# Startup and weight-split order in a four-layer SSM/SwiGLU kernel: input loaded first, sines last, and a rewritten row at the end of the kernel stage

## The chip, the cores and the metric

The kernel runs on one core of one Trainium2 chip. The metric is the device time of one execution in microseconds. The kernel before took 1164.55 us, the median of 3 runs (1164.26 to 1165.54).

## The reference

Four layers follow one another on an activation of 2048 rows by 512 channels. Layers 1 and 3 are a state-space convolution, layers 2 and 4 a SwiGLU block; both layers of a kind share their weights.

```python
def _A_ref(u, A_re, A_im, B_re, B_im, C_re, C_im, log_dt, Dskip):
    dt = jnp.exp(log_dt)[:, None]
    logdA = dt * (A_re + 1j * A_im)
    P = jnp.exp(logdA[:, :, None] * l[None, None, :])
    K = jnp.einsum("dn,dnl,dn->dl", Cc, P, dt * Bc).real
    ...
    y = irfft(rfft(u padded) * rfft(K padded))[:L] + u * Dskip
def _B_ref(x, w_gate, w_up, w_down):
    return (_silu(x @ w_gate) * (x @ w_up)) @ w_down
x = x + _A_ref(_layernorm(x), ...)
x = x + _B_ref(_layernorm(x), ...)
x = x + _A_ref(_layernorm(x), ...)
x = x + _B_ref(_layernorm(x), ...)
```

## The kernel before

The program has three parts.

**Startup.** `dt` is the exponential of `log_dt`, made by a polynomial on VectorE (DVE) over 4 columns, spread to all partitions by a diagonal matrix `dg` (L169), one matrix product `pd` (L170) and a copy on ScalarE (ACT, L172). `rho` (L958) is `dt` times the real part of A. The phases are kept as turns: `turn_units` (L373) scales the imaginary part (L379), rounds it on ACT (L380) and subtracts (L382); it runs once for the first 64 channels (`first`) and once for the other 448 (`others`). For one chunk of 64 channels `gen_turns` (L387) makes the phases by shifts and additions, `gen_trig` (L404) their sines and cosines on ACT (`re`, `im`), `gen_exp` (L416) the 25 exponentials `mz` and `re[:, a]`, and `gen_g` (L456) and `gen_e` (L441) multiply these into the two factors of the convolution kernel. `stats` (L196) makes mean and variance of the 4 row groups of block 0 of the input (`xne`) with BN_STATS, the power -0.5 on GpSimd (POOL), and `norm_early` (L287) normalizes them on ACT. `direct` (L292) is the forward transform of a block as fp32 matrix products (L298).

**Kernel stage.** For each of 8 chunks of 64 channels, 128 small products `pk` (`lags`, L498) make the convolution kernel, which is copied (`ks`, L509), spread over the partitions (for the last two chunks by `kp`, L525, on TensorE), given the skip term (`skip`, L505), and transformed into spectra (`spectra`, `first_parts` L582, `later_parts` with the products of L533). At its end stand, for the last chunk, the first convolution block and the preparation of the SwiGLU weights. `ssm_half` (L740) is a generator for one half of the channels: four steps, each a spectrum product on DVE (`yk` L778, `yf` L783 and L784) and an inverse transform on PE (`pi`, L798), with the sums `bb` (L750 on ACT, L758 and L759 on DVE), and two final steps that add the results to the residual rows `xg` (L812 to L831). `conv[0]` and `conv[1]` are the two halves of block 0. `split_weights` (L647) yields for each of 11 weight pieces a load into a staging tile, a `hi` step (fp16 copy on ACT, L666 or L691) and a `lo` step (the fp16 rest on DVE, L671 or L694); `tags` names the staging buffer of each load, where a number is a third of a not yet used weight buffer. `split(hi, lo, load)` takes the next ones of each list. `scales` (L344) computes the power-of-two scales from the largest squares. `second` (L306) is the transform of block 1 by `direct`. `first_norm` (L832) normalizes and transposes (`pt`, L845) the first 256 rows for the SwiGLU block.

**SwiGLU and convolution blocks.** For 8 pairs of layer and block, gate and up products `pgu` (L911 to L914: three fp16 products for each fp32 one, two buffers of PSUM), the gate's SiLU on ACT (L917), the product with up on DVE (L918, `sg`), and the down products `py` (L926 to L928), while DVE, ACT and PE work on the convolution of the next block. The order here is found by the scheduler of the framework, from its own estimates.

In the first two parts the rows of ACT, DVE, PE and POOL are in the order in which the code is written (`manual_schedule`); the DMA queue of SyncE (SP) is put in order by the scheduler at both ends. Each engine takes its row in order, so that an instruction which waits holds up all behind it.

Of the kernel before, what the change touches and what calls it, by code (L numbers as in the profile page):

```python
# [22 lines left out]
P = 128  # L23
# [4 lines left out]
HD = D // 2  # L28
# [46 lines left out]
def kernel(ctx, tc, x, a_re, a_im, b_re, b_im, c_re, c_im, log_dt, d_skip,  # L75
                           w_gate, w_up, w_down, c_ef, c_ei, c_ek, c_am, c_eh, c_eih, out):
    nc = tc.nc
    V, A, G, PE = nc.vector, nc.scalar, nc.gpsimd, nc.tensor
# [9 lines left out]
    def tl(shape, name, tag, dt=F32):  # L88
        return sb.tile(shape, dt, name=name, tag=tag, bufs=BUFS[tag])
# [17 lines left out]
    def load_half(c):  # L107
        nc.sync.dma_start(xe[:, c:c + 2], x[0, c * P:(c + 2) * P, :].rearrange("(c p) d -> p c d", p=P))
    load_half(0)
    rho = load(a_re, "rho", "u")  # L110
    th = load(a_im, "th", "u")
    am = sb.tile([P, NA], I32, name="am")
    nc.sync.dma_start(am, c_am)
    load_half(2)
    bw = tl([P, 2, D], "bw", "nn")
    br, bi = bw[:, 0], bw[:, 1]
    nc.sync.dma_start(br, b_re)
# [75 lines left out]
        V.tensor_reduce(dmax, da, axis=AX.X, op=OP.max)  # L193


    def stats(src, rows, scale, tag="stats", between=None, then=None):  # L196

        st = tl([P, 4, 6], "st", tag)
        mv = tl([P, 4, 2], "mv", tag)
        rs = tl([P, 8], "rs", tag)  # L200
        nb = rs[:, 4:]
        for r in range(rows):
            if between and r == 2:
                between()
            V.bn_stats(st[:, r], src[:, r])
            V.bn_aggr(mv[:, r], st[:, r])
        V.tensor_scalar(rs[:, :rows], mv[:, :rows, 1], EPS, 1.0 / scale ** 2, OP.add, OP.mult)
        G.tensor_tensor(rs[:, :rows], rs[:, :rows], mhalf[:, :rows], OP.pow)
        if then:
            then()  # L210
        V.scalar_tensor_tensor(nb[:, :rows], mv[:, :rows, 0], -1.0, rs[:, :rows], OP.mult, OP.mult)
        return rs, nb
# [191 lines left out]
    def gen_trig(ts):  # L404


        re, im, mu, xz, mz = ts
        A.activation(xz[:, 2], xz[:, 1].bitcast(I32), AF.Sin, scale=-TWO_PI / TURN)
# [222 lines left out]
    def take(it, n):  # L631
        for _ in range(n):
            next(it, None)
# [13 lines left out]
    def split_weights():  # L647


        cb = F // 4  # L650
        tags = iter(("bt", 0, 1, 2, "bt", 0, 1, 2, "n", "xf", "bt"))

        def columns(j, wi, src):
            fs = slice(j * cb, (j + 1) * cb)
# [298 lines left out]
    with tc.manual_schedule(engines={mybir.EngineType.Activation, mybir.EngineType.DVE, mybir.EngineType.PE, mybir.EngineType.Pool}):  # L953
# [3 lines left out]
        def turns():  # L957
            V.tensor_tensor(rho, rho, dt, OP.mult)  # L958
            take(first, 1)
            take(ex, 14)  # L960
            take(others, 1)
            take(first, 1)
            take(gen_turns(0, ts[0]), 7)
        ft = tl([P, 2, 2, D], "ft", "ga")
        first, others = turn_units(ft, 0, DC), turn_units(ft, DC, D)
        stats_x = stats(xe, 4, 1.0, between=turns, then=lambda: take(others, 1))
        tr = gen_trig(ts[0])
        take(tr, 2)
        norm_early(xe, ne, stats_x)
        gen_w()  # L970
        take(ex, 11)
        fw = [direct(0, h, q, [ne[:, c, h * HD:(h + 1) * HD] for c in range(4)]) for h in range(2) for q in QORD]
        for f in fw:
            next(f)
# [171 lines left out]
        xg = tl([P, 2, 4, D], "xg", "gb")  # L1146
        xs[0], xs[1] = xg[:, 0], xg[:, 1]
        wsl += [tl([P, 6 * F], f"wsl{k}", f"W{k}", F16) for k in range(4)]
        load_x(xs[0], 0, 0)
        split(0, 0, 3)  # L1150
        conv = [ssm_half(0, 0, h) for h in range(2)]

        def slots():
# [2 lines left out]
            yield from itertools.cycle([w[:, j] for w in (wz, wm) for j in range(2)])  # L1156
        slots = slots()

        ks = spread_in(pk)
        odd = later_parts(c - 1, kts[0], (3, 1))  # L1160
        rest = later_parts(c, kts[1])
        bb1 = tl([P, 2, 2, 2, HD], "bb1", "n")
        norm = first_norm(tl([P, 2, D], "nn1", "hf"))
        take(conv[0], 1)
        spread_pe(ks, kts[1])
        skip(c, kts[1], V)
        take(conv[0], 1)
        scales()
        split(1, 0)
        first_parts(c, 0)  # L1170
        take(conv[0], 1)
        split(1, 1)
        split(0, 0, 1)
        first_parts(c - 1, 3)
        split(1, 0)
        take(conv[0], 1)
        first_parts(c - 1, 1)
        split(1, 0)
        take(conv[1], 1)
        first_parts(c, 2)  # L1180
        take(conv[1], 1)
        split(0, 1)
        split(0, 0, 1)
        take(conv[0], 1)
        take(conv[1], 1)
        split(1, 1)
        split(0, 0, 1)
        take(conv[1], 1)
        split(0, 1)
        split(0, 0, 1)  # L1190
        take(odd, 2)
        take(conv[1], 1)
        take(norm, 1)
        take(rest, 2)
        take(odd, 1)
        take(norm, 1)
# [11 lines left out]
        take(rest, 3)  # L1208
        split(1, 1)
        take(rest, 4)  # L1210
        split(0, 0, 3)
        sizes(c, kts[1], ks)
        direct_size()
        nn2 = tl([P, 2, D], "nn2", "nn")
        take(second(*sec[-1]), 2)
    pscale = product_scale()
    with tc.high_priority(offset=BOOST // 2):
        while los:
# [50 lines left out]
```

## Time and profile before

| quantity | value |
|---|---|
| median of 3 runs | 1164.55 us |
| the profiled execution | 1163.83 us |
| its span in the trace | 1161.1 us |
| around the span | 2.7 us |
| mean granted TensorE clock | 0.989 |
| first `pk` product | 56.55 us |
| last `pk` product ends, first `pi` starts | 258.5 us |
| first gate product | 318.53 us |

The page gives the busy time of each engine, the timeline the single instructions in order of time (start, length, engine, line, operation; in brackets the idle time before it and what ended it), and the list of waits who waited for whom. A row with "x4" merges four instructions. PE is TensorE.

### The profile page before, as it was taken

To read this page: it belongs to the slowest core of one execution; us is meant where nothing else is said; L and a number is where in the kernel's file an instruction comes from. 1 tells how busy PE (TensorE), PEld (TensorE's weight loads), DVE (VectorE), ACT (ScalarE), POOL (GpSimd) and SP (SyncE) were. 2 spreads that over 40 slices of the span, in tenths; PEclk is the share of its full clock that TensorE was granted. 3 is DMA by queue.
4 is the path that set the end of the run, shared out by engine and by line. 5 is a ranking of instruction groups with operands and counts; after the bars stand their busy time and mean duration, and the time that the engine had idled before them with its cause. 6 is when DMAs were issued, how large, how long until landed. Compare 5 with 4: busy or idle time off the path is not lost.

```text
span 1161.1 us, 24400 instructions
## 1 busy us (share of the span) xinstructions
PE 1101.9 (95%) x9942; PEld 877.3 (76%) x9942; DVE 998.6 (86%) x1586; ACT 599.7 (52%) x1198; POOL 109.7 (9%) x162
## 2 busy tenths in 40 slices
PE   2989999998889999999999999999999999999998
PEld 1868888886776868687868687868777686876875
DVE  7999999968789999999899999989994999983212
ACT  6889898733553463557453533655433452334211
POOL 1112222210000010010010000210000010000000
PEclk9989999998899999999999999999999999999999
DMA  5357677866394437332264444343534145312000
GB/s 208 129 162 164 161 178 175 187 172 226 112 289 119 145 119 222 105 111 74 79 155 134 127 161 145 103 132 88 164 109 150 49 121 158 102 42 46 15 23 19
DMA packets 127314, 150.38 MB, mean 130 GB/s; under 512 B 50897, under 2 KB 75985, under 8 KB 127202
## 3 DMA queue, kind: packets, MB, share of 16 engines
q1 hardware_dynamic: 115298, 123.32, 34.9%
q0 software_dynamic: 11904, 25.50, 9.5%
q8 instruction: 78, 1.28, 0.5%
q14 instruction: 34, 0.28, 0.1%
HBM read 98.70 MB, written 33.82 MB: 114 GB/s over the span
## 4 chain that ended last, share of the span: by engine, by line
DVE 30%; PE 30%; issue 7%; DMA 4%; ACT 3%; SPq 1%; POOL 1%; DVEq 0%; ACTq 0%; POOLq 0%
PE pgu L911 5%; PE pgu L912 5%; PE pgu L914 5%; DVE t L778 5%; DVE yk L781 4%; PE py L926 3%; PE py L927 3%; PE py L928 3%; DVE yk L778 3%; DVE z L230 3%; DVE sg L918 2%; PE pi L798 2%; PE pf L282 2%; DVE hl L920 2%; DMA w<-wdr 2%
## 5 line engine op out<-in xcount | busy, mean ns | idle before, releaser
L911 PE MATMUL pgu<-mix,wsl 128*128 128x256 f16 x1280 | 299.2, 273 | 5.5 <-DVE sg L918 5.0
L912 PE MATMUL pgu<-mix,wsl 128*128 128x256 f16 x1280 | 298.9, 273 | 0.0
L914 PE MATMUL pgu<-mix,wsl 128*128 128x256 f16 x1280 | 195.2, 273 | 0.0
L912 PEld LDWEIGHTS <-wsl 128*128 128x128 f16 x1280 | 125.2, 98 | 22.7 <-issue 6.4
L926 PE MATMUL py<-wsl,hh 128*128 128x512 f16 (+1 forms) x352 | 133.5, 379 | 4.9 <-DVE xg L931 3.0
L911 PEld LDWEIGHTS <-wsl 128*128 128x128 f16 x1280 | 125.1, 98 | 16.4
L914 PEld LDWEIGHTS <-wsl 128*128 128x128 f16 x1280 | 125.2, 98 | 15.3
L928 PE MATMUL py<-wsl,hl 128*128 128x512 f16 (+1 forms) x352 | 133.4, 379 | 0.5 <-DVE hl L920 0.5
L927 PE MATMUL py<-wsl,hh 128*128 128x512 f16 x320 | 121.3, 379 | 0.0
L778 DVE TENSOR_TENSOR t<-uu,w 128x1024 f32<-128x1024 f32 x96 | 116.9, 1218 | 3.5 <-DMA w<-wdr 3.2
L917 ACT ACTIVATE sg<-pgu,sc 128x512 f32<-128x512 f32 x80 | 54.6, 683 | 125.1 <-PE pgu L914 121.8
L781 DVE TENSOR_TENSOR yk<-yk,t 128x1024 f32<-128x1024 f32 x96 | 116.8, 1217 | 0.2
L918 DVE SCALAR_TENSOR_TENSOR sg<-pgu,sc,sg 128x512 f32<-128x512 f32 x80 | 59.6, 745 | 52.1 <-ACT sg L917 51.9
L533 PE MATMUL pw<-kt,ek 128*128 128x256 f32 (+1 forms) x384 | 92.2, 378 | 0.0
L919 ACT ACTIVATE hh<-sg 128x512 f16<-128x512 f32 x80 | 50.1, 627 | 79.5 <-DVE sg L918 79.5
L533 PEld LDWEIGHTS pw<-kt,ek 128*128 128x128 f32 x384 | 73.6, 196 | 8.6
L798 PE MATMUL pi<-yl,mix 128*128 128x256 f16 x576 | 78.9, 273 | 0.6 <-DVE yl L230 0.3
L282 PE MATMUL pf<-z,eh 128*128 128x256 f16 x576 | 74.9, 273 | 0.6 <-DVE z L230 0.6
L778 DVE TENSOR_TENSOR yk<-u,w0r 128x1024 f32<-128x1024 f32 x56 | 68.1, 1217 | 0.8 <-ACT u L284 0.8
L498 PE MATMUL pk<-re,g 128*32 128x64 f32 x1024 | 65.1, 317 | 3.6 <-DMA g<-g 1.9
L920 DVE TENSOR_TENSOR hl<-sg,hh 128x512 f16<-128x512 f32 x80 | 54.9, 686 | 15.5 <-ACT hh L919 15.4
L927 PEld LDWEIGHTS <-hh 128*128 128x128 f16 (+1 forms) x352 | 34.4, 98 | 41.6 <-issue 6.0
(237 smaller groups left out, 2165.9 us busy)
## 6 DMA issues: line engine op xcount, KB each, us to landing
w<-wdr SPq DMA_DIRECT2D x96, 256.0 KB, 2.7
uu<-udr SPq DMA_DIRECT2D x96, 256.0 KB, 3.0
udr<-u POOLq DMA_DIRECT2D x32, 256.0 KB, 2.6
g<-g POOLq DMA_DIRECT2D x6, 1024.0 KB, 9.1
udr<-u SPq DMA_DIRECT2D x16, 256.0 KB, 3.0
n<-xdr SPq DMA_DIRECT2D x4, 1024.0 KB, 5.7
kdr<-ks SPq DMA_DIRECT2D x6, 512.0 KB, 2.6
kt<-kdr SPq DMA_DIRECT2D x24, 128.0 KB, 2.9
```

The source lines that it names most:

```text
L282: PE.matmul(pf[:, o], lhsT=e, rhs=m, start=k == 0, stop=k == len(terms) - 1)
L533: PE.matmul(pw[:, i], lhsT=e, rhs=kt[:, :, c + 4 * k0:4 * k1:4, :].rearrange("p g k d -> p k g d"), start=c == 0, stop=c == 3)
L778: V.tensor_tensor(t, uu.unsqueeze(2).to_broadcast([P, NQ, 2, 2, DC]), w.unsqueeze(3).to_broadcast([P, NQ, 2, 2, DC]), OP.mult)
L781: V.tensor_tensor(yk, yk, t, OP.add)
L798: PE.matmul(pi[:, o], lhsT=e, rhs=m, start=k == 0, stop=k == len(terms) - 1)
L911: PE.matmul(o, lhsT=wgu(wi, k, 0)[:, fs], rhs=nh[:, k], start=k == 0, stop=False)
L912: PE.matmul(o, lhsT=wgu(wi, k, 1)[:, fs], rhs=nh[:, k], start=False, stop=False)
L914: PE.matmul(o, lhsT=wgu(wi, k, 0)[:, fs], rhs=nlo[:, k], start=False, stop=k == 3)
L918: V.scalar_tensor_tensor(sg, pgu[:, 1], sc6[:, 4:5], sg, OP.mult, OP.mult)
L926: PE.matmul(py[:, r], lhsT=hh[:n, f, rc], rhs=wd(f, 0)[:n], start=f == 0, stop=False)
L927: PE.matmul(py[:, r], lhsT=hh[:n, f, rc], rhs=wd(f, 1)[:n], start=False, stop=False)
L928: PE.matmul(py[:, r], lhsT=hl[:n, f, rc], rhs=wd(f, 0)[:n], start=False, stop=f == FT - 1)
```

## The change

Six things are changed, and none adds or drops arithmetic.

1. The second half of block 0's rows is loaded right behind the first, ahead of `rho`, `th` and `am`.
2. `stats` no longer breaks off after two row groups; all four BN_STATS come first and `turns` is called while POOL takes the power.
3. In `turns` all 25 exponentials of chunk 0 are taken at once, and the large part of `turn_units` is begun only behind `gen_turns`. Then come the normalization, `gen_w`, the sines of chunk 0, and the last step of `others`.
4. The staging buffers of the weight loads are dealt out otherwise (the second load gets `n` instead of a third of a weight buffer).
5. `scales` and the first `hi` step stand ahead of the copy of the last `pk`, and the first two pieces' `lo` steps are between the first convolution steps; the others come later than before. The skip term of the last chunk is added on POOL instead of DVE.
6. The last transform of block 1 (`second(*sec[-1])`, 8 products and their copy) stands ahead of the last convolution step instead of at the end of the stage.

```diff
     load_half(0)
+    load_half(2)
     rho = load(a_re, "rho", "u")
...
-    load_half(2)
...
-    def stats(src, rows, scale, tag="stats", between=None, then=None):
+    def stats(src, rows, scale, tag="stats", then=None):
...
-            if between and r == 2:
-                between()
...
-        tags = iter(("bt", 0, 1, 2, "bt", 0, 1, 2, "n", "xf", "bt"))
+        tags = iter(("bt", "n", 0, 1, "bt", 2, 0, 1, "n", "xf", "bt"))
...
         def turns():
             V.tensor_tensor(rho, rho, dt, OP.mult)
             take(first, 1)
-            take(ex, 14)
-            take(others, 1)
+            take(ex, 25)
             take(first, 1)
             take(gen_turns(0, ts[0]), 7)
+            take(others, 1)
...
-        stats_x = stats(xe, 4, 1.0, between=turns, then=lambda: take(others, 1))
-        tr = gen_trig(ts[0])
-        take(tr, 2)
+        stats_x = stats(xe, 4, 1.0, then=turns)
         norm_early(xe, ne, stats_x)
         gen_w()
-        take(ex, 11)
+        take(gen_trig(ts[0]), 2)
+        take(others, 1)
...
+        split(0, 0, 1)
         load_x(xs[0], 0, 0)
-        split(0, 0, 3)
+        split(0, 0, 2)
...
+        scales()
+        split(1, 0)
         ks = spread_in(pk)
...
-        take(conv[0], 1)
-        spread_pe(ks, kts[1])
-        skip(c, kts[1], V)
-        take(conv[0], 1)
-        scales()
-        split(1, 0)
-        first_parts(c, 0)
-        take(conv[0], 1)
-        split(1, 1)
-        split(0, 0, 1)
-        first_parts(c - 1, 3)
+        last = second(*sec[-1])
         split(1, 0)
         take(conv[0], 1)
-        first_parts(c - 1, 1)
-        split(1, 0)
-        take(conv[1], 1)
-        first_parts(c, 2)
-        take(conv[1], 1)
+        split(0, 1)
+        split(0, 0, 1)
+        spread_pe(ks, kts[1])
+        skip(c, kts[1], G)
+        take(conv[0], 1)
         split(0, 1)
         split(0, 0, 1)
         take(conv[0], 1)
+        first_parts(c, 0)
+        split(1, 0)
+        bb1 = tl([P, 2, 2, 2, HD], "bb1", "n")
+        first_parts(c - 1, 3)
+        take(conv[0], 1)
+        first_parts(c - 1, 1)
         take(conv[1], 1)
-        split(1, 1)
-        split(0, 0, 1)
+        first_parts(c, 2)
+        split(1, 0)
         take(conv[1], 1)
-        split(0, 1)
-        split(0, 0, 1)
+        take(conv[0], 1)
+        take(conv[1], 1)
+        split(1, 0)
+        take(last, 2)
+        take(conv[1], 1)
         take(odd, 2)
         take(conv[1], 1)
         take(norm, 1)
+        split(0, 0, 1)
+        split(0, 1)
+        split(0, 0, 1)
...
+        split(0, 1)
         split(0, 0, 3)
...
-        take(second(*sec[-1]), 2)
```

What stands in the rows of the engines, in the built programs (lines of the kernel after are two or three less from L205 on). First ACT at the start, before: `mz` and `re<-rho` are exponentials, `re<-im`, `im<-im` and `re<-re,hpi` the large sines and cosines of chunk 0, `xne` the normalization of block 0.

```order
L426 ACTIVATE re<-rho 128x64 x9
L380 ACTIVATE ft<-ft 128x2x448
L408 ACT_TABLE_LOAD
L408 ACTIVATE xz<-xz 128x320
...
L411 ACTIVATE re<-im 128x2048
L412 ACTIVATE im<-im 128x2048
L413 ACTIVATE re<-re,hpi 128x2048
L290 ACTIVATE xne<-xne,rs 128x512 x4
L426 ACT_TABLE_LOAD
L426 ACTIVATE re<-rho 128x64 x11
```

The same place of ACT's row after:

```order
L424 ACTIVATE re<-rho 128x64 x20
L378 ACTIVATE ft<-ft 128x2x448
L288 ACTIVATE xne<-xne,rs 128x512 x4
L406 ACT_TABLE_LOAD
L406 ACTIVATE xz<-xz 128x320
...
L409 ACTIVATE re<-im 128x2048
L410 ACTIVATE im<-im 128x2048
L411 ACTIVATE re<-re,hpi 128x2048
```

Eleven exponentials and the four normalizations have moved ahead of the sines, and one table load is gone here (a second one is gone ahead of the sines of chunk 1).

DVE behind the last `wo` of the kernel stage (L565, the end of chunk 6's spectrum sums), before: `sc` is the last result of `scales`, and the rows of L671 are `lo` steps.

```order
L565 TENSOR_TENSOR wo<-pw,wo 128x2x6x64
L778 TENSOR_TENSOR yk<-mix,w0r 128x1024
L783 TENSOR_TENSOR yf<-yk 128x256
L784 TENSOR_TENSOR yf<-yk 128x256
L505 TENSOR_TENSOR kt_429<-kt_429,tdk 1x4x16
L778 TENSOR_TENSOR yk<-mix,w0r 128x1024
L783 TENSOR_TENSOR yf<-yk 128x256
L784 TENSOR_TENSOR yf<-yk 128x256
L346 TENSOR_REDUCE c_2718<-cmx 128x3
```

And after, where the eleven small steps of `scales` are cut to their first and last:

```order
L563 TENSOR_TENSOR wo<-pw,wo 128x2x6x64
L344 TENSOR_REDUCE c_2674<-cmx 128x3
...
L356 TENSOR_SCALAR sc_92<-bits 128x6
L776 TENSOR_TENSOR yk<-mix,w0r 128x1024
L781 TENSOR_TENSOR yf<-yk 128x256
L782 TENSOR_TENSOR yf<-yk 128x256
L669 SCALAR_TENSOR_TENSOR wsl_2665<-st_2533,sc_92,wsl_2665 128x2x344
L669 SCALAR_TENSOR_TENSOR wsl_2666<-st_2533,sc_92,wsl_2665 128x2x344
L776 TENSOR_TENSOR yk<-mix,w0r 128x1024
L781 TENSOR_TENSOR yf<-yk 128x256
L782 TENSOR_TENSOR yf<-yk 128x256
L669 SCALAR_TENSOR_TENSOR wsl_2667<-st_2669,sc_92,wsl_2666 128x4x344
```

The skip term (L505) has left DVE's row, and `scales` and the `lo` steps of two pieces stand where DVE had waited behind it.

Last, DVE where the SwiGLU products begin. `wx` is the last piece of the down weights, `t<-uu,w` the first product of block 1 with stored spectra, and `sg` the first gate product. Before:

```order
L694 SCALAR_TENSOR_TENSOR wx<-st_3029,sc_92,wsl_2668 96x512
L694 SCALAR_TENSOR_TENSOR wsl_2667<-st_3025,sc_92,wsl_2667 128x512
L778 TENSOR_TENSOR t<-uu,w 128x1024
L694 SCALAR_TENSOR_TENSOR wsl_2667<-st_3025,sc_92,wsl_2667 128x512
L694 SCALAR_TENSOR_TENSOR wsl_2668<-st_3025,sc_92,wsl_2667 128x512
L694 SCALAR_TENSOR_TENSOR wsl_2668<-st_3025,sc_92,wsl_2668 128x512
L781 TENSOR_TENSOR yk<-yk,t 128x1024
L918 SCALAR_TENSOR_TENSOR sg_3072<-pgu,sc_92,sg_3072 128x512
```

After:

```order
L193 TENSOR_REDUCE dmax<-da 1x1
L776 TENSOR_TENSOR t<-uu,w 128x1024
L692 SCALAR_TENSOR_TENSOR wsl_2668<-st_3042,sc_92,wsl_2668 128x512 x2
L692 SCALAR_TENSOR_TENSOR wx<-st_3042,sc_92,wsl_2668 96x512
L916 SCALAR_TENSOR_TENSOR sg_3073<-pgu,sc_92,sg_3073 128x512
```

The first gate product now stands ahead of eight of the eleven `lo` steps of the down weights. From here on the scheduler has sorted all rows anew: on PE the first inverse transform of block 1 stands behind 177 gate and up products, before behind 127.

More of the change, by code (lines that the diff above doesn't have):

```diff
@@ L1161 @@
         rest = later_parts(c, kts[1])
-        bb1 = tl([P, 2, 2, 2, HD], "bb1", "n")
         norm = first_norm(tl([P, 2, D], "nn1", "hf"))
-        take(conv[0], 1)
-        spread_pe(ks, kts[1])
-        skip(c, kts[1], V)
-        take(conv[0], 1)
-        scales()
-        split(1, 0)
-        first_parts(c, 0)
-        take(conv[0], 1)
-        split(1, 1)
-        split(0, 0, 1)
-        first_parts(c - 1, 3)
+        last = second(*sec[-1])
         split(1, 0)
         take(conv[0], 1)
-        first_parts(c - 1, 1)
-        split(1, 0)
-        take(conv[1], 1)
-        first_parts(c, 2)
-        take(conv[1], 1)
+        split(0, 1)
[3 more added lines that the diff above has]
+        take(conv[0], 1)
         split(0, 1)
```

## Prediction

> **What bounds the kernel now.** I read the page first.
>
> ```profile
> span 1161.1 us, 24400 instructions
> PE 1101.9 (95%) x9942; PEld 877.3 (76%) x9942; DVE 998.6 (86%) x1586; ACT 599.7 (52%) x1198; POOL 109.7 (9%) x162
> ```
>
> PE and DVE are both nearly full, so an average decides nothing. Busy time by stretches of the span says where there is room (stretch, length, busy PE, PEld, DVE, ACT, POOL, clock, DMA share, GB/s):
>
> ```profile
> 250.00:264.00 14.00, 12.39 (x298) 10.54 (x296) 3.91 (x7) 3.71 (x6) 0.00 (x0) 1.00 0.59 164
> 297.00:319.00 22.00, 17.39 (x93) 16.85 (x94) 15.53 (x34) 13.16 (x34) 1.35 (x1) 0.84 0.26 76
> 345.00:600.00 255.00, 250.45 (x2108) 194.35 (x2107) 244.71 (x438) 131.01 (x260) 24.95 (x30) 1.00 0.42 125
> 600.00:1161.00 561.00, 552.99 (x4599) 422.59 (x4598) 442.84 (x704) 219.76 (x419) 29.23 (x38) 1.00 0.34 100
> ```
>
> From 600 us on PE is busy 98.6% and DVE 79%: a PE that comes earlier ends earlier. From 345 to 600 both are full (PE 98.2%, DVE 96%). In the first stretch DVE works 3.9 of 14 us, in the second PE and DVE are both partly idle. The lists of waits of DVE and of PE around the end of the kernel stage say for what (waiting line, awaited, us in all, times, longest):
>
> ```profile
> DVE kt L505 <- ACT kt L527: 9.5, 1, 9.5
> DVE wos L602 <- ACT wos L601: 4.1, 1, 4.1
> DVE t L778 <- DMA w<-wdr: 2.6, 1, 2.6
> DVE mix L602 <- ACT mix L601: 2.2, 1, 2.2
> ...
> PE pt L845 <- ACT nn L843: 5.3, 1, 5.3
> PE pgu L911 <- DVE sg L918: 4.6, 1, 4.6
> ```
>
> So DVE stands 9.5 us behind the skip term while PE makes the last `pk`, and PE later waits twice for what DVE and ACT then have left over.
>
> **Startup: +4.3 us.** Here DVE sets the end. The timeline:
>
> ```profile
> 6.11 0.66 DVE L205 BATCH_NORM_STATS2 st<-xne 128x6 f32<-128x512 f32 x1
> 11.69 0.31 ACT L380 ACTIVATE ft<-ft 128x128 int32<-128x128 f32 x1 [1.03 <-DVE ft L379]
> 12.64 1.41 ACT L426 ACTIVATE re<-rho 128x64 f32<-128x64 f32 x9
> 12.65 0.28 DVE L382 TENSOR_TENSOR ft<-ft 128x128 f32<-128x128 f32 x1
> 13.95 0.93 ACT L380 ACTIVATE ft<-ft 128x896 int32<-128x896 f32 x1
> 14.90 1.28 ACT L408 ACT_TABLE_LOAD   x1
> 16.20 0.47 ACT L408 ACTIVATE xz<-xz 128x320 f32<-128x320 int32 x1
> 16.57 0.69 DVE L205 BATCH_NORM_STATS2 st<-xne 128x6 f32<-128x512 f32 x1
> 23.52 2.92 ACT L290 ACTIVATE xne<-xne,rs 128x512 f32<-128x512 f32 x4
> 26.40 0.29 DVE L464 TENSOR_TENSOR g<-w,re 128x128 f32<-128x128 f32 x1
> 56.55 0.50 PE L498 MATMUL pk<-re,g 128*32 128x64 f32 x8 [1.75 <-DVE re L453]
> ```
>
> The first `pk` waited for DVE (last row), and from 11 to 56 us DVE's row has no other wait than 0.2 us for POOL. L464 multiplies by `re[:, 64]`, the last of the sines, so it can't start before ACT's last sine. Before, the sines ended at 23.5 and DVE came at 26.40. After, ACT's chain is: two more BN_STATS stand in DVE's row ahead of `dg`, 0.6 us each by the start of the next instruction, so everything behind `dt` is 1.15 late and the small L380 runs at 12.85 to 13.15. Then 25 exponentials at 0.146 (nine in the 1.31 from 12.64 to 13.95) take until 16.8; the large L380 now waits for DVE, where L382 to the end of `gen_turns` takes 3.92 (12.65 to 16.57) from 13.15 on and the two large scalings about 1.0, so until 18.1. Then 0.93, the normalization 2.92, the table load 1.30 (14.90 to 16.20) and all sines 7.32 (16.20 to 23.52): 30.6. DVE, which has done `gen_w` and the rest meanwhile, waits there some 4.5 us and takes L464 at 30.65 instead of 26.40: **+4.25**. All rows of DVE behind it are as before until the end of chunk 6, with ACT's next sines hardly later than before, so the whole kernel stage shifts by it. The two BN_STATS that leave the loaded part (1.7 us) gain nothing, since what they free is spent in that wait. PE's direct transforms, that start some 4 us earlier, end long before the first `pk` either way. Two table loads less make ACT shorter by 2.6, which is in the chain already as far as it counts. The bounds: +3.0, if the large scalings and L380 overlap better than I take it, and +5.5, if the second half of the input, which is needed before `dg` now, holds up the BN_STATS and so `dt`.
>
> The Trainium skill (ScalarE: Activation LUTs, What ACT_TABLE_LOAD costs) gives a load and a drain, 2.66 us for a switch; the trace shows 1.30 from the load's start to the next activation. By the page the two loads that go would be worth 5.3 us of ACT instead of 2.6, and the sum would be the same, because the path runs through the one load that stays.
>
> **End of the kernel stage: first gate product 10.6 us earlier.** All clocks here are those of before, without the 4.25.
>
> ```profile
> 258.53 1.99 PE L798 MATMUL pi<-yf,mix 128*128 128x256 f32 x8
> 260.45 1.94 PE L525 MATMUL kp<-ks,ident 128*32 128x256 f32 x32
> 268.72 0.55 PE L582 MATMUL pw<-kt,ef 128*128 128x64 f32 x4
> 270.45 1.95 PE L798 MATMUL pi<-yf,mix 128*128 128x256 f32 x8
> 272.23 0.61 PE L582 MATMUL pw<-kt,ef 128*128 128x128 f32 x4
> 281.29 0.43 DVE L813 TENSOR_TENSOR t<-bb 128x256 f32<-128x256 f32 x1
> 283.69 1.22 DVE L778 TENSOR_TENSOR yk<-mix,w0r 128x1024 f32<-128x1024 f32 x1
> 297.03 0.69 DVE L205 BATCH_NORM_STATS2 st<-xg 128x6 f32<-128x512 f32 x1
> 301.61 1.97 PE L845 MATMUL pt<-ident,nn 128*128 128x128 f32 x8 [5.30 <-ACT nn L843]
> 303.37 0.85 PE L533 MATMUL pw<-kt,ef 128*128 128x192 f32 x2
> 305.93 0.54 PE L533 MATMUL pw<-kt,ef 128*128 128x192 f32 x2
> 307.28 0.49 PE L533 MATMUL pw<-kt,ef 128*128 128x192 f32 x2
> 315.08 0.60 PE L298 MATMUL pf<-n,ef 128*128 128x256 f32 x2
> 318.53 0.27 PE L911 MATMUL pgu<-mix,wsl 128*128 128x256 f16 x1
> ```
>
> DVE fills its 9.5 us with `scales`, two convolution steps and the `lo` steps of the first piece. Then PE is the bound from 258.5 on: eight `pi` and four `first_parts` at 1.75 (268.72, 270.45, 272.23), `kp` 1.95 and the direct transform of block 1, 3.45 (315.08 to 318.53), make 26.4. I add 1.8 for two waits of PE: DVE is held once by the second `hi` step (ACT takes it only behind `ks`), once by the input of the second half, whose loads now stand on SP's queue behind four weight loads. The last `pi` ends at 286.7; DVE adds 1.3 for its sums and 2.4 (281.29 to 283.69) for the first rows: norm at 290.5 instead of 297.0. From norm to `pt` I take 5.2 (4.6 before), as another `lo` step is in between: 295.7 instead of 301.6, **-5.9**. From `pt` to the first gate product it took 16.92: 1.76, the first pair of L533 products at 2.56, seven at 1.3, and the 3.45 of L298. The 3.45 has moved ahead (**-3.45**); the slow pair, behind 5.3 us of idle PE, costs 1.26 more than its followers, and I take that as gone, PE's idle time being 3.8 now (**-1.26**). So 307.9: **-10.6**. Moving the skip term to POOL costs nothing as long as it takes less than what DVE's 0.2 us leaves: PE reaches the products that need it only behind two `pi`. POOL's rows bound it by 0.1 (a memset) and 1.7 (the power).
>
> The Trainium skill (TensorE: Matmul & The Clock Gate, What's actually happening) lets the array fall to half rate after an idle window of about 3.4 us; the slow pair agrees with that. By that rule 3.8 us of idle time can still cost the pair, and the sum would be 1.3 us worse.
>
> **What is left of it behind the first gate products: 1.4 us less.** Before, PE waited 4.6 at the third group for the first `sg`:
>
> ```profile
> 322.30 4.40 ACT L691 ACTIVATE wsl<-st,sc 128x512 f16<-128x512 f32 x7 [1.53 <-DMA st<-in_B_w_down_dram]
> 333.77 0.37 PE L911 MATMUL pgu<-mix,wsl 128*128 128x256 f16 x1 [4.59 <-DVE sg L918]
> 334.23 0.74 DVE L918 SCALAR_TENSOR_TENSOR sg<-pgu,sc,sg 128x512 f32<-128x512 f32 x1
> ```
>
> After, the first `sg` needs only three L691 ahead of it on ACT, but DVE has two more weight pieces' `lo` steps between norm and first product. Walking DVE's new row with these durations the first `sg` ends at 320.8 and the second at 328.1, against 318.4 and 326.1 at which PE would want them: two waits of 2.4 and 2.1, the same 4.6 together. So PE keeps its lead of 10.6 there. DVE's lead is less: its waits from 252 to the second `sg` were 9.5, 4.1, 2.2, 1.1 and some 1 in small ones, 18; mine are 1.9, 2.1, 2.6, 3.0 and 1.5, so 11, a lead of 7. PE's lead is cut between 0 and 3.6 by it in the following 200 us, where DVE is as full as PE; I take 1.4, nearer to 0, because on PE the first transform of block 1 now stands 50 gate products (5.4 us) later, so that DVE has room.
>
> **The sum** against the profiled execution: 1163.83 + 4.25 - 10.6 + 1.4 = 1158.9. The median of the runs is 0.7 above the profiled one; I predict **1159**.
>
> **The rivals.**
>
> *DVE's lead alone is carried.* Then -7 + 4.25: 1161.1; with a slow pair behind `pt` at most 1162.4. For it: DVE 96% busy from 345 to 600. Against it: PE's new row.
>
> *Slower: DVE loses its lead at block 1's spectra.* The load of `w`, for which DVE waited 2.6 us at 338 before, now feeds an instruction that stands ahead of the first `sg` (L776 after). If that wait comes there, and the waits for ACT at the `wos` and `mix` sums stay at 4.1 and 2.2 instead of my 3.0 and 1.5, the lead falls from 7 to 2.6. As soon as it is below the 4.25 of the startup, the kernel gets slower: +1.7, 1165.5, and more if the scheduler's new order of the blocks adds waits of PE (PE is idle for 4.6 us of the stretch from 345 to 600 and for 8.0 behind it, 12.6 together).
>
> *The startup doesn't slow down.* If L464 came at 26.4 after all, -9.2: 1154.6. Against it: only ACT's last sine can release it, and that chain has no slack.
>
> *The change doesn't do what it says*, in that loading all input first moves nothing: before, no row waited for the second half (16.57 has none), so by itself it gives 0; this is inside the forecast.
>
> **How the numbers follow.** My forecast has a chance of 0.43 (1157 to 1161.5), DVE's lead alone 0.21, slower 0.24, no startup loss 0.12. About 0.2%, 2.3 us, is what a measurement of this kernel can tell from no change: 1162.2 and 1166.9 are the borders. Faster is the forecast, the last case and a third of the second: 0.62. Slower by over 2.3 us is the larger part of its rival: 0.19, since the scheduler's new order can only add to its 1165.5; the rest, 0.19, is the same. The range reaches from the startup at +3.0 with both waits for `sg` gone (1152) to the slower case with the slow pair behind `pt` as well (1167).
>
> **What would show it.** Right: a DVE wait of 4 to 5 us at the first product of `g` with ACT's sine as its releaser, the first `pk` near 61; no wait for the skip term at the end of the stage; first gate product at 307.9 + 4.25 = 312; waits for `sg` of 2 us, not of 4.6. Wrong: a first `pk` near 56; `pi` products that wait for loads of `mix`; a first gate product behind 316; or more than 20 us of idle PE behind 345.

## The result

The changed kernel takes 1171.52 us (median of 5 runs, 1169.06 to 1174.31) against 1164.55: 1.0063 of before, with a 95% interval of 1.0043 to 1.0083. It is slower by 7 us, where the prediction had it faster by 5.6.

The profiled execution of the kernel after has this span and these busy times (the page's first lines):

```profile
span 1169.4 us, 24402 instructions
PE 1100.0 (94%) x9942; PEld 876.1 (75%) x9942; DVE 999.2 (85%) x1585; ACT 598.2 (51%) x1196; POOL 107.5 (9%) x163
```

PE and DVE work as long as before within 2 us (1101.9 and 998.6). So the 8.3 us by which the span is longer are idle time of both, and the question is where the two wait.

### The profile page after: what moved, and what is told of

It is laid out like the page before. It is cut to its first block, busy times and chain, and to the rows that moved or that the text cites. A ratio compares the mean times of both kernels' runs of the same rounds, so it can differ in the third digit from the quotient of the medians.

```text
span 1169.4 us, 24402 instructions
## 1 busy us (share of the span) xinstructions
PE 1100.0 (94%) x9942; PEld 876.1 (75%) x9942; DVE 999.2 (85%) x1585; ACT 598.2 (51%) x1196; POOL 107.5 (9%) x163
## 4 chain that ended last, share of the span: by engine, by line
PE 48%; DVE 30%; issue 11%; DMA 7%; ACT 3%; POOL 1%; SPq 1%; DVEq 0%; POOLq 0%; ACTq 0%
PE pgu L909 7%; PE pgu L910 7%; PE pgu L912 7%; PE pw L531 4%; DVE yk L779 4%; DVE t L776 4%; PE py L924 4%; PE pi L796 4%; PE py L925 3%; PE py L926 3%; DMA g<-g 3%; PE pf L280 3%; PE pk L496 3%; DVE yk L776 3%; PE pk L497 2%
## 5 line engine op out<-in xcount | busy, mean ns | idle before, releaser
L912 PEld LDWEIGHTS <-wsl 128*128 128x128 f16 x1280 | 125.4, 98 | 14.8
L531 PE MATMUL pw<-kt,ek 128*128 128x256 f32 (+1 forms) x384 | 91.8, 376 | 0.0
L531 PEld LDWEIGHTS pw<-kt,ek 128*128 128x128 f32 x384 | 73.5, 196 | 8.5
L496 PE MATMUL pk<-re,g 128*32 128x64 f32 x1024 | 65.1, 317 | 13.5 <-DVE re L451 10.5
L918 DVE TENSOR_TENSOR hl<-sg,hh 128x512 f16<-128x512 f32 x80 | 54.8, 686 | 16.3 <-ACT hh L917 16.2
```

What stands on the lines that cost most here:

```text
L496: PE.matmul(o, lhsT=g[:, 0, :, d], rhs=re[:, 0:64, d], start=True, stop=False, tile_position=(0, 32 * grp))
L531: PE.matmul(pw[:, i], lhsT=e, rhs=kt[:, :, c + 4 * k0:4 * k1:4, :].rearrange("p g k d -> p k g d"), start=c == 0, stop=c == 3)
L912: PE.matmul(o, lhsT=wgu(wi, k, 0)[:, fs], rhs=nlo[:, k], start=False, stop=k == 3)
```

## The profile after, in the order of the prediction's steps

**Startup.** The timeline of the kernel after, for DVE's first product of `g` and the first `pk`:

```profile
30.73 0.29 DVE L462 TENSOR_TENSOR g<-w,re 128x128 f32<-128x128 f32 x1 [4.48 <-ACT re L411]
60.82 0.50 PE L496 MATMUL pk<-re,g 128*32 128x64 f32 x8 [10.53 <-DVE re L451]
```

DVE waits 4.48 for ACT's last sine and starts at 30.73, where 30.65 was predicted; the first `pk` is 4.27 later than before (4.25).

**End of the kernel stage.** The timeline of PE from the last `pi` but one to the first gate products:

```profile
284.46 1.99 PE L796 MATMUL pi<-yf,mix 128*128 128x256 f32 x8 [1.21 <-DVE yf L781]
286.29 0.59 PE L296 MATMUL pf<-n,ef 128*128 128x256 f32 x2
...
289.75 1.89 PE L796 MATMUL pi<-yf,mix 128*128 128x256 f32 x8
...
300.13 1.36 PE L843 MATMUL pt<-ident,nn 128*128 128x128 f32 x8 [3.30 <-ACT nn L841]
301.33 0.70 PE L531 MATMUL pw<-kt,ef 128*128 128x192 f32 x2
...
303.75 0.85 PE L531 MATMUL pw<-kt,ef 128*128 128x192 f32 x2
...
313.42 0.27 PE L909 MATMUL pgu<-mix,wsl 128*128 128x256 f16 x1
...
325.88 0.27 PE L909 MATMUL pgu<-mix,wsl 128*128 128x256 f16 x1 [1.82 <-DVE sg L916]
...
333.12 0.27 PE L909 MATMUL pgu<-mix,wsl 128*128 128x256 f16 x1 [1.84 <-DVE sg L916]
```

Without the startup's 4.27 the first gate product stands at 309.15, 9.4 earlier than before (predicted 10.6), and PE waits twice for `sg`, 1.82 and 1.84 (predicted 2.4 and 2.1). With the startup counted, the kernel after leads by 5.1 us at the first gate product (313.42 against 318.53). The transform of block 1 (`pf`, L296) now stands between two `pi`.

**Behind the first gate products.** The list of DVE's waits from 330 to 470 us (waiting line, awaited, us in all, times, longest), first of before:

```profile
DVE t L778 <- DMA w<-wdr: 3.2, 3, 2.6
DVE bb L758 <- PE pi L798: 0.9, 1, 0.9
DVE hl L920 <- ACT hh L919: 0.7, 1, 0.7
DVE z L230 <- ACT z L272: 0.4, 1, 0.4
```

Then of after:

```profile
DVE t L776 <- DMA w<-wdr: 5.8, 2, 3.8
DVE nn L862 <- DMA mix<-nn: 2.1, 1, 2.1
DVE rs L224 <- POOL rs L223: 1.8, 1, 1.8
DVE hl L918 <- ACT hh L917: 1.4, 2, 0.7
DVE z L228 <- ACT z L270: 0.9, 1, 0.9
```

DVE waits 12.2 instead of 5.2 us (a row of 0.2 after is left out). For PE the same list sums to 13.6 instead of 6.5. Before, nearly three quarters of it are the waits for `sg` that the prediction names:

```profile
PE pgu L911 <- DVE sg L918: 4.8, 2, 4.6
```

These are PE's largest waits after:

```profile
PE pgu L909 <- DVE xg L929: 2.6, 2, 1.4
PE pi L796 <- ACT yl L785: 2.5, 1, 2.5
PE pi L796 <- DVE yf L781: 2.4, 2, 1.3
PE pi L796 <- DVE yl L228: 2.3, 1, 2.3
```

Of the 13.6 us, 11.1 are PE behind DVE and 2.5 PE behind ACT; without the waits for `sg` it is 11.8 against 1.7. To the waits comes slow work behind them: in the stretch in which PE waits 2.3 and 2.5 us for `yl`, the mean granted clock is 0.93, where it was 1.00 before (stretch, length, busy PE, PEld, DVE, ACT, POOL, clock, DMA share, GB/s; first before, then after):

```profile
400.00:450.00 50.00, 49.09 (x413) 37.23 (x411) 49.93 (x86) 26.99 (x52) 6.76 (x7) 1.00 0.43 125
400.00:450.00 50.00, 43.04 (x326) 30.29 (x324) 47.20 (x85) 23.98 (x48) 4.77 (x8) 0.93 0.51 157
```

From the lead of 5.1 us at the first gate product to the 8.3 behind at the end, 13.4 us are lost. By the busy times of the stretches PE is idle 7.7 us more than before between 330 and 470 us (13.6 against 5.9) and 2.6 more behind 470 (13.2 against 10.6). Of the other 3 us an estimated 2 are slower work between 330 and 470 us: the granted clock in its two halves of 70 us is 1.00 and 0.95, where it was 0.98 and 1.00.

## The experiments

Theory A: the startup costs its 4.3 us, and the end of the stage gains what was predicted, but the order in which the scheduler sorts everything behind the first gate product takes more than the gain back; what decides there is DVE's waiting, not PE's start. Its rivals are in the expectations.

The table sums the lists of waits of DVE over two stretches and of PE over the second. The ratio is that to the kernel before on the same chip, with its 95% interval; the kernel before took between 1164.2 and 1166.0 us on these chips, so kernels of different chips are better compared by their ratios.

| kernel | median us | ratio | first pk | first gate product | DVE waits 252-330 | DVE waits 330-470 | PE waits 330-470 |
|---|---|---|---|---|---|---|---|
| before | 1164.55 | 1 | 56.55 | 318.53 | 17.2 | 5.2 | 6.5 |
| after | 1171.52 | 1.0063 (1.0043-1.0083) | 60.82 | 313.42 | 13.5 | 12.2 | 13.6 |
| 1 startup only | 1169.98 | 1.0036 (1.0026-1.0047) | 61.14 | 323.96 | 20.3 | 5.6 | 7.2 |
| 2 end only | 1167.69 | 1.0021 (1.0010-1.0032) | 56.53 | 310.03 | 12.4 | 11.9 | 11.7 |
| 3 after, transform at the end | 1161.34 | 0.9962 (0.9947-0.9977) | 61.40 | 314.88 | 10.9 | 5.6 | 3.7 |
| 4 after, buffers of before | 1178.32 | 1.0107 (1.0087-1.0128) | 60.60 | 316.26 | 16.3 | 10.0 | 11.1 |
| 5 end only, transform at the end | 1156.93 | 0.9928 (0.9915-0.9942) | 56.26 | 310.40 | 9.6 | 5.9 | 4.1 |
| 6 before, transform ahead | 1173.21 | 1.0071 (1.0059-1.0084) | 56.64 | 317.64 | 18.5 | 9.5 | 8.9 |
| 7 after, normalization behind sines | 1172.09 | 1.0061 (1.0049-1.0073) | 58.86 | 311.67 | 14.8 | 11.3 | 12.4 |
| 8 after, loads of w first | 1170.34 | 1.0051 (1.0037-1.0065) | 60.98 | 313.32 | 13.0 | 12.4 | 9.8 |
| 9 after, useless products | 1167.80 | 1.0023 (1.0012-1.0034) | 60.90 | 316.53 | 13.1 | 8.6 | 8.7 |
| 10 after, skip term on DVE | 1178.02 | 1.0098 (1.0082-1.0113) | 60.57 | 317.17 | 17.3 | 12.2 | 12.9 |
| 11 load order alone | 1165.23 | 1.0003 (0.9993-1.0012) | 56.53 | 318.37 | 16.6 | 5.4 | 7.1 |
| 12 end only, transform in PE's gap | 1164.59 | 0.9989 (0.9976-1.0001) | 56.55 | 305.00 | 7.8 | 12.7 | 12.2 |

### 1 and 2: the two halves of the change

The first kernel is before with edits 1 to 3 (startup), the second before with edits 4 to 6 (weights and end of the stage), each as in the diff above. The main lines of the first are

```diff
-            take(ex, 14)
-            take(others, 1)
+            take(ex, 25)
...
+        stats_x = stats(xe, 4, 1.0, then=turns)
         norm_early(xe, ne, stats_x)
         gen_w()
+        take(gen_trig(ts[0]), 2)
```

and of the second

```diff
-        skip(c, kts[1], V)
+        skip(c, kts[1], G)
...
+        take(last, 2)
...
-        take(second(*sec[-1]), 2)
```

Expected of the first:

> The kernel before with the three startup edits alone; the end of the kernel stage is as before, and PE's row behind the first gate product is nearly that of before (the first four pi behind 123 gate products instead of 127). Theory A (the startup costs the 4.3 us by which the first pk moves, and the rest of the loss comes from the end of the stage): 1164.6 + 4.3 = 1168.8, first pk near 60.8, PE's waits behind the first gate product as before. Rival C (the startup has all of the loss, by side effects in the kernel stage): 1171.5. Rival D (the SwiGLU part takes up the 4.3 us, since PE's waits there shrink): 1164.6.

Expected of the second:

> The kernel after with the startup of before: from the first pk on, PE's row is word for word that of the kernel after. Theory A: 1171.5 - 4.3 = 1167.2, first pk near 56.6, first gate product near 309.2, and still some 10 us more of PE's waits behind it than before. Rival C: 1164.6. Rival of the forecast on record (the end of the stage gains and the loss needs the startup): 1155.

The startup alone costs 4.9 us, with the first `pk` 4.6 later, as theory A has it (C and D fall). The end alone costs 2.6, although its first gate product comes 8.5 earlier than before (theory A again; the forecast's 1155 and C fall). So each half is slower by itself, and the second half is where the prediction went wrong: 11 us are lost behind 310 us.

### 3, 5 and 6: the place of the last transform of block 1

The third kernel is after with edit 6 undone:

```diff
-        last = second(*sec[-1])
...
         split(1, 0)
-        take(last, 2)
         take(conv[1], 1)
...
         nn2 = tl([P, 2, D], "nn2", "nn")
+        take(second(*sec[-1]), 2)
```

> The kernel after, with the last transform of block 1 back at the end of the stage. PE's row behind the first gate product is then close to that of before (first pi behind 136 products instead of 177), and on SP's queue three loads of w stand ahead of the transposing DMAs of hh and hl instead of two. Theory A (the new order behind the first gate product takes DVE's lead, mainly by its waits for w and nn): the first gate product comes some 3.4 us later than in the kernel after, near 316.8, but DVE waits at most 3 us for w instead of 5.8, and DVE's lead of 5.9 us is carried: 1163 to 1166. Rival B (DVE's lead is lost whatever the order, because DVE's row is full there): 1171 to 1175.

It came out at 1161.34, 10 us below after and 3.8 below before. That is faster than theory A's 1163 to 1166, and the first gate product comes 1.9 earlier than expected (314.88); rival B falls. DVE's waits from 330 to 470 us are back at 5.6. The same edit with the startup of before, so edits 4 and 5 alone, is the fifth kernel:

> The startup of before, and the end of the stage of after with the last transform of block 1 back at its end. Theory A (the startup costs 4.3 to 4.9 us and the place of that transform some 10, and the two add up): 1161.3 - 4.6 = 1156.7, first pk near 56.6, DVE's waits from 252 to 800 us as in the kernel of the third experiment (29 us). Rival (what the startup loses is taken up by waits further on): 1161.

1156.93 was measured where 1156.7 was expected, so startup and transform add up; this is the fastest of all kernels, 0.9928 of before. The list of DVE's waits from 330 to 470 us in it:

```profile
DVE nn L864 <- DMA mix<-nn: 2.0, 1, 2.0
DVE t L778 <- DMA w<-wdr: 1.6, 2, 1.0
DVE rs L226 <- POOL rs L225: 0.9, 1, 0.9
```

Its waits for `w` and for POOL are a third and a half of those of after. The sixth kernel makes edit 6 alone, on before:

```diff
+        last = second(*sec[-1])
...
         split(1, 1)
         split(0, 0, 1)
+        take(last, 2)
         take(conv[1], 1)
...
-        take(second(*sec[-1]), 2)
```

> The kernel before with edit 6 alone: the last transform of block 1 stands ahead of a convolution step instead of at the end of the stage. PE's first four pi of block 1 then stand behind 144 gate and up products instead of 127. Theory A (the place of this transform by itself makes the part behind the first gate product lose): PE is idle for 10 us or more from 333 to 470 us instead of 6.5, 1169 to 1175. Rival B (it loses only together with the other edits of the end): 1162 to 1166.

It costs 9 us by itself (1173.21, theory A; B falls); PE waits 8.9 us from 330 to 470, a little less than the 10 expected. One part of the cost is seen directly. In the list of DVE's waits from 252 to 330 us of the sixth kernel stands

```profile
DVE bb L758 <- PE pi L798: 2.5, 1, 2.5
```

and the same 2.5 stand in the lists of the kernel after and of the second, where before, the third and the fifth kernel have no such row: the last `pi` stands behind the 3.45 us of the transform, and DVE waits for it. And the first gate product gains next to nothing: 310.03 with the transform ahead (second kernel), 310.40 with it at the end (fifth).

### 12: the transform where PE is idle

The twelfth kernel is the second with the transform behind the last `pi`:

```diff
-        take(last, 2)
         take(conv[1], 1)
         take(odd, 2)
         take(conv[1], 1)
+        take(last, 2)
         take(norm, 1)
```

> The startup of before and the end of the stage of after, with the last transform of block 1 moved three places further back: behind the last convolution step and ahead of pt, where PE is idle for 3.3 to 3.7 us anyway. It so costs PE nothing and DVE doesn't wait for a pi behind it, and the first gate product should come near 307, some 3 us earlier than in the second and fifth experiments. But the rows of PE, DVE and ACT behind it are again those of the second experiment (first pi behind 177 gate and up products). Theory A (the order behind the first gate product costs some 7 us, the wait of DVE for the last pi 2.5): only the 2.5 come back, 1163 to 1166, with DVE's waits from 333 to 470 us at 11 or 12. Rival (the order is harmless and an earlier first gate product is carried): 1153 to 1157.

Its PE around `pt` and at the first gate product:

```profile
293.40 1.36 PE L845 MATMUL pt<-ident,nn 128*128 128x128 f32 x8 [0.27 <-ACT nn L843]
294.60 0.49 PE L533 MATMUL pw<-kt,ef 128*128 128x192 f32 x2
...
295.90 0.49 PE L533 MATMUL pw<-kt,ef 128*128 128x192 f32 x2
...
305.00 0.27 PE L911 MATMUL pgu<-mix,wsl 128*128 128x256 f16 x1
```

The first gate product comes at 305.00, 5.4 us ahead of the fifth kernel, and DVE has waited 1.8 less by 330 us. Yet the kernel takes 1164.59, 7.7 more than the fifth (7.1 by the ratios, as the two ran on different chips). This is theory A's range, and the rival (1153 to 1157) falls. The list of DVE's waits from 330 to 470 us:

```profile
DVE t L778 <- DMA w<-wdr: 6.0, 2, 3.9
DVE nn L864 <- DMA mix<-nn: 2.6, 1, 2.6
DVE rs L226 <- POOL rs L225: 1.7, 1, 1.7
```

These are the waits of the kernel after, with the order of the kernel after (first `pi` behind 177 gate and up products). From 252 to 800 us DVE waits 35.8 us in the twelfth and 28.4 in the fifth kernel, 7.4 more. As DVE works equally long in both, its idle time has to differ by about what the time differs by; the lists say where that idle time lies (6.8 of it from 330 to 470 us), not why. That the order is the cause follows from the pair of kernels: with the same work and an earlier start of PE and DVE, the order behind it, of the engines and of SP's queue, is what is left to make the end later. Against the second kernel, whose order it shares, the twelfth gains 3.1 (3.7 by the ratios), where the wait for the last `pi` was 2.5.

### 9: useless work

```diff
         nn2 = tl([P, 2, D], "nn2", "nn")
+        take(second(*sec[-1]), 1)
```

> The kernel after, with the eight products of the last transform of block 1 made a second time at the end of the stage, into a PSUM tile that nobody reads: 3.45 us of useless work on PE ahead of the first gate product. The scheduler, which now reckons with a later PE, puts the first pi of block 1 behind 135 gate and up products, as in the third experiment, instead of 177. Theory A (the plan of the scheduler behind the first gate product costs the 7 us that DVE waits more from 333 to 470 us, and PE has time to spare there): DVE's waits in that stretch fall from 12.2 to 5 or 6 us, and the kernel gets faster by useless work, 1164 to 1167. Rival B (the order is harmless, and PE's row sets the time): 1171.5 + 3.5 = 1175. Rival C (what helps at the end is only that DVE no longer waits 2.5 us for the last pi): no change, 1171.5.

1167.80, just above the range of theory A: 3.7 us faster than after by 3.45 us more work on PE. B and C fall. DVE's waits from 330 to 470 us went from 12.2 to 8.6, where 5 or 6 had been expected: the order is another one than that of the kernel after, but not that of the third either. DVE's wait for the last `pi` is still there, and the first gate product is 3.1 later.

### 8: is it the load of w?

In the kernel after, SP's queue has these issues one behind the other (a DMA's own time there is that of its issue):

```profile
348.42 2.40 SPq L890 DMA_TRANSPOSE hh<-sg  x2
350.91 2.46 SPq L890 DMA_TRANSPOSE hl<-sg  x2
353.46 0.53 SPq L772 DMA_DIRECT2D w<-wdr  x1
```

and DVE waits for what the last of them brings:

```profile
358.22 1.22 DVE L776 TENSOR_TENSOR t<-uu,w 128x1024 f32<-128x1024 f32 x1 [3.81 <-DMA w<-wdr]
```

So the eighth kernel brings the loads of `w` forward:

```diff
-                    nc.sync.dma_start(w, wdr[k, h, q])
+                    with tc.high_priority(offset=2 * BOOST):
+                        nc.sync.dma_start(w, wdr[k, h, q])
```

> The kernel after, with the loads of w at the highest priority for the scheduler: on SP's queue the third load of w stands behind one of the four transposing DMAs of hh and hl instead of behind all four; the other engines' rows are the same until some 450 instructions into DVE's convolution of block 1. Theory A1 (DVE's waits for w are what the new order costs): DVE's wait of 3.8 us for w near 358 us falls below 1, and 1167 to 1169. Rival A2 (those waits take no time that PE would not lose anyway, since the first pi stand too late): 1171.

DVE's waits from 330 to 470 us are then

```profile
DVE nn L863 <- DMA mix<-nn: 4.9, 2, 3.3
DVE bb L756 <- PE pi L797: 4.6, 3, 2.4
DVE t L777 <- DMA w<-wdr: 1.4, 3, 0.8
DVE rs L224 <- POOL rs L223: 1.3, 1, 1.3
```

The wait for `w` has gone from 5.8 to 1.4, and the sum stays at 12.4 (12.2): DVE now waits for PE's `pi` and for the transposed rows instead. The time is 1170.34, within the scatter of after: A1 falls, and A2's time fits. So this late load alone is not the cause. Up to 352 us DVE's row is that of the kernel after, and there already the next links are late: 3.3 us instead of 2.1 for the transposed rows, 1.5 instead of none for a `pi`. From there on the scheduler has put DVE's row in another order too, so how much of the later waits belongs to that order isn't shown.

### 4, 10, 7 and 11: other parts of the change

The fourth kernel takes edit 4 back:

```diff
-        tags = iter(("bt", "n", 0, 1, "bt", 2, 0, 1, "n", "xf", "bt"))
+        tags = iter(("bt", 0, 1, 2, "bt", 0, 1, 2, "n", "xf", "bt"))
```

> The kernel after with the staging buffers dealt out as before, nothing else. The scheduler then puts the first four pi behind 144 products instead of 177, and the third load of w ahead of the transposing DMAs of hh and hl. Theory A: first gate product as in the kernel after (313 to 314, or later if the second weight load has to wait for its buffer), DVE's waits for w under 3 us, 1164 to 1168. Rival B: 1171 to 1174.

It was slower still, 1178.32; both expectations missed. In its waits of ACT from 252 to 275 us stands a new one,

```profile
ACT wsl L664 <- DMA wsl<-in_B_w_up_dram: 3.2, 1, 3.2
```

so it seems that the second `hi` step, that early, needs the new buffer for its load. The order behind, though its first `pi` stand behind 144 products only, has 10.0 us of DVE's waits from 330 to 470. The number of products ahead of the first `pi` is thus no measure of what an order costs. But the trace is that of the fastest of this kernel's runs (1174.17), and it has a loss of its own much later: PE is idle for 8.4 us from 800 to 1000, where all other kernels have 1.2 to 2.8. What put it there is not known.

The tenth kernel has the skip term on DVE:

```diff
-        skip(c, kts[1], G)
+        skip(c, kts[1], V)
```

> The kernel after with the skip term on DVE as before; every other row of PE and DVE is the same up to the end of the kernel stage and far beyond it. Forecast on record (moving it costs nothing as long as POOL is quick enough): DVE waits for kt some 0 to 2 us, since the lo steps now fill the time, and 1171.5 within 1. Rival (the move to POOL is what fills DVE's 9.5 us): some 5 to 8 us slower, 1177 to 1179.

1178.02, 6.5 more than after (4.1 by the ratios), so the rival is nearer than the forecast of no change; behind some 394 us DVE's row is again in an order of its own, which may have a share in it. DVE's row:

```profile
267.78 0.21 DVE L503 TENSOR_TENSOR kt<-kt,tdk 1x64 f32<-1x64 f32 x1 [6.04 <-ACT kt L525]
```

`scales` and the `lo` steps that now stand ahead of it fill only a third of the 9.5 us of before; the rest ends because the skip term has left DVE's row.

The seventh kernel moves the normalization behind the sines:

```diff
-        norm_early(xe, ne, stats_x)
         gen_w()
         take(gen_trig(ts[0]), 2)
+        norm_early(xe, ne, stats_x)
```

> The kernel after with the normalization of block 0 behind the sines of chunk 0 on ACT; PE's row is that of the kernel after up to its 3131st instruction. Startup theory (DVE's first product of g waits for ACT's last sine, so each us ahead of it on ACT counts): the sines end 2.92 earlier, first pk 60.8 - 2.9 = 57.9, and 1171.5 - 2.9 = 1168.6 if the rest passes it on. Rival (the path goes through DVE's or POOL's part of the startup): first pk near 60.8 and 1171.5.

In its startup DVE's first product of `g` and PE's last direct transform stand at

```profile
27.64 0.29 DVE L462 TENSOR_TENSOR g<-w,re 128x128 f32<-128x128 f32 x1 [2.02 <-ACT re L411]
...
57.48 1.46 PE L296 MATMUL pf<-xne,ek 128*128 128x256 f32 x6
58.86 0.49 PE L496 MATMUL pk<-re,g 128*32 128x64 f32 x8
```

DVE comes 3.09 earlier, so the sines do release it; but PE's direct transforms, which start later, now end at 58.86 without a pause, and 1.96 of it arrive at the first `pk`, between the two expectations. The first gate product is 1.75 earlier than after, and the time is the same as after (1172.09), though not for the rival's reason: the rows are other ones again from PE's 3131st instruction on, and PE's waits from 470 to 800 us grow from 5.4 to 9.1.

The eleventh kernel is edit 1 alone, with every other row as before:

```diff
     load_half(0)
+    load_half(2)
...
-    load_half(2)
```

> The kernel before with edit 1 alone (the second half of block 0's rows loaded right behind the first); the rows of PE, DVE and ACT are word for word those of before. Forecast on record: 0, so 1164.6 within 0.7, first pk at 56.6. Rival (the 512 kB ahead of rho, th and am hold up rho's or the turns' loads): first pk later by up to 1.5, 1166.

1165.23, ratio 1.0003 (0.9993 to 1.0012), first `pk` at 56.53: nothing, as predicted.

## Why the prediction was wrong

**Startup, +4.25: right.** 4.27 in the profile, 4.9 as a kernel of its own, 4.4 between the third and the fifth kernel (4.0 by their ratios). One remark beside it doesn't hold: with a dearer table load the sum would not have been the same, since one load stands in ACT's chain (21.98 to 23.27, 1.29 us) and DVE waits for the end of that chain.

**Load first, 0: right** (experiment 11). **Skip term on POOL at no cost: right** (POOL takes 0.54 us for it, and nobody waits), but incomplete: the working had DVE fill the 9.5 us with moved steps, and without the move to POOL 6.0 of them stay (experiment 10).

**First gate product, -10.6: nearly right (-9.4), with one term wrong.** Without the 4.27, `pt` stands at 295.86 where 295.7 was predicted. Some luck is in that: the norm came 0.8 later than predicted, and from the norm to `pt` it took 4.55 instead of 5.2. From `pt` to the first gate product the working had 12.2, and it took 13.29. The slow pair of products behind `pt` was taken as gone, its idle time being 3.8; with 3.30 it is still there (last section). Moving the transform is worth next to nothing here, by the working itself (its 3.45 leave the way behind `pt`, and stand in PE's row ahead of the last `pi` instead) and by the runs (0.4 between the second and the fifth kernel).

**"What is left of it behind the first gate products: 1.4 us less": this step failed.** 13.4 us were lost there (a lead of 5.1 at the first gate product, 8.3 behind at the end). I carried PE's lead through and let DVE's smaller lead cut it a little; the working even took the later place of the first transform on PE as room for DVE. The runs show the opposite. In the new order DVE itself waits 7 us more from 330 to 470 us, and PE then waits for DVE (11.1 of its 13.6 us). The twelfth kernel separates this from everything else: 5.4 us ahead of the fifth at the first gate product, 7.7 behind it at the end. The ninth shows that the order changes with the work that is put on PE ahead of it: useless work made the kernel 3.7 us faster. And the last line of the sum is 0.6 too low by its own terms, 1158.9 and 0.7 being 1159.6, which changes nothing here.

**The rivals.** The one on the other side was the right kind (DVE loses its lead at block 1's spectra, and the scheduler's new order adds waits of PE), with too small a price: 4.4 us of DVE's lead, instead of 7 in its waits from 330 us on. Its condition did not come true as stated: the product ahead of the first `sg` waits for no load, and the waits at the `wos` and `mix` sums are 2.0 and 2.7. The waits for `w` came at 358 and 390 us (3.8 and 2.0), and they are only one link, as the eighth kernel shows. "More than 20 us of idle PE behind 345" was named as the sign of a wrong forecast, and the kernel after has 23.7 (11.0 and 12.7 of these two stretches):

```profile
345.00:600.00 255.00, 244.00 (x1980) 188.27 (x1978) 238.06 (x428) 124.99 (x251) 21.08 (x29) 0.99 0.40 121
600.00:1169.40 569.40, 556.69 (x4649) 426.08 (x4646) 448.23 (x712) 224.81 (x424) 30.09 (x38) 1.00 0.34 101
```

**What stays open:** which single exchange of instructions makes the order bad. In all fourteen kernels the orders with the transform ahead have 9.5 to 12.7 us of DVE's waits from 330 to 470 us (8.6 with the useless products), and those with it at the end 5.2 to 5.9; why just these is not shown. Orders that differ further back move PE's waits from 470 to 800 us between 3.8 and 9.1, so differences of 2 or 3 us between kernels whose orders differ shouldn't be read as effects of an edit.

## What to carry to other kernels

Where a scheduler sorts a part by its own estimates, a piece of work moved ahead of that part changes two things, and the second, the new order, can cost more than the first gains: compare the waits of the fullest engines over the first 100 us or so behind the seam, not the time at which it is reached. A lead of one engine is lost where it soon waits for another that is as full, as PE did for DVE here. Look too at who waits for what the moved work is put ahead of: 3.45 us on PE ahead of the last `pi` made DVE wait 2.5. And try each half of such a change alone: here the best kernel is one half of it, with one of its moves taken back.

## What was unexpected of the hardware

The granted TensorE clock fell after shorter pauses than the 3.8 us at which the prediction took the slow pair as gone. Behind 3.30 us of idle PE ahead of `pt` the kernel after has these granted clocks (the number ahead of the last two):

```profile
300.00:302.00 2.00, 1.82 (x11) 1.58 (x12) 1.26 (x2) 1.25 (x3) 0.00 (x0) 0.87 0.76 202
302.00:304.00 2.00, 2.00 (x8) 2.00 (x7) 0.56 (x1) 2.00 (x6) 0.00 (x0) 0.50 0.90 229
```

The first group of L531 products took 2.42 us (301.33 to 303.75) instead of 1.30, and the drop began after PE had started again (1.00 from 300 to 301 us, 0.74 in the next). In the twelfth kernel, with 0.27 us of idle time, the same group took 1.30 (294.60 to 295.90). Before, even pauses of 2.99 and 2.48 us did it: the timeline of PE of the kernel before has

```profile
265.38 3.51 PE L798 MATMUL pi<-yf,mix 128*128 128x256 f32 x8 [2.99 <-DVE yf L783]
...
285.42 5.69 PE L798 MATMUL pi<-yf,mix 128*128 128x256 f32 x16 [2.48 <-DVE yf L783]
```

Eight products behind the first pause took 3.51 instead of the 1.95 of the next eight (270.45, in the prediction's rows), and sixteen behind the second 5.69 instead of twice that: 3.4 us of slow work for 5.5 of waiting. The granted clock was 0.50 from 265.4 to 267 us and 0.51 from 287 to 289. Behind the 1.21 us in the kernel after (284.46, above) there is no such loss, nor behind its waits of 1.82 and 1.84 for `sg` (clock 1.00); behind its 2.33 us for `yl` (420 us) the clock is 0.50 from 421 to 424.

The Trainium skill (TensorE: Matmul & The Clock Gate, What's actually happening) has the array at half rate after at least one idle window of about 3.4 us. The half rate agrees with the 0.50 here; the length does not, as pauses of 2.33 to 3.30 us were enough. In these kernels a wait of PE of 2.3 to 5.3 us cost more than its length, and one that was filled gave more back.

A transposing DMA of `hh` or `hl` takes 1.2 us of SP's queue by its issue (2.40 and 2.46 for two), two to four times as much as the loads of `w` around them (0.32 to 0.57), so the four of them delay what is queued behind by 5 us.
